# Attention with a split-precision score product: transposing q and k in float32 and splitting behind the transpose

## The chip, the cores and the metric

The kernel runs on one core of a Trainium2 chip. The core has five engines that run side by side and wait for each other by semaphores: TensorE (PE: matrix products, with its weight loads shown as PEld), VectorE (DVE), ScalarE (ACT), GpSimd (POOL) and SyncE (SP), which here only issues DMAs. Products land in PSUM, which only PE, DVE and ACT reach. The metric is the device time of one execution in microseconds, as the median of several runs; lower is better. A trace of one profiled execution shows when each instruction ran.

## The reference

Four sequences of 768 positions, eight heads of 64. Each position attends to the `n_global` = 8 first keys and to the `n_local` = 96 last ones, with a bias per head that falls with the distance; the result of all heads goes through a feed-forward network (FFN) with a rational function in the middle.

```python
scores = scale * np.matmul(q, k.transpose(0, 1, 3, 2))
keep = is_global | is_local          # key < 8, or 0 <= query - key < 96
bias = -slopes[:, None, None] * dist[None, :, :]
scores = np.where(keep, scores + bias, -1e9)
a = np.exp(scores - np.max(scores, axis=-1, keepdims=True))
a = a / (np.sum(a, axis=-1, keepdims=True) + 1e-09)
x = np.matmul(a, v)                  # heads side by side: 3072 tokens x 512
h = x @ w_in                         # 512 -> 2048
P = a[0] + a[1] * h + a[2] * h**2 + a[3] * h**3
Q = 1.0 + np.abs(b[0]) * np.abs(h) + np.abs(b[1]) * h**2
out = (P / (Q + 1e-06)) @ w_out      # 2048 -> 512
```

All data are float32; the weights arrive as 64-bit numbers and are decoded on the chip.

## The kernel before, in words

**Units and steps.** Attention is cut into 96 units (`unit`): 128 queries of one sequence and two heads, so four units to a block of 128 tokens. A window of 96 keys reaches no further back than the block before, so a unit's keys are its own block and the one before it (256 columns, in two halves of `kT` used in turn); the eight global keys are written over the first columns of the older half (`kG`, L409). The first block of a sequence, i = 0, has one half only. The FFN goes in chunks of 256 tokens, eight parts `f` to a chunk. The loop in `windowed` (L511) makes 110 steps `t`; each step takes up pieces of several units and FFN parts, with the FFN twelve steps behind (`LAG`) and its second product two more (`F2`). Within a step the order is set by the numbers in `PRI` and `PRI_A` (lower is earlier): scores 50, softmax 100, first half of the first FFN product 150, transposes of q and k 200, product with v 250, and so on. A scheduler turns these priorities and the dependencies into one instruction order per engine. Pairs of units share a load (`st_load`, every even step, two pairs ahead) and the product with v (`st_pv`, odd steps).

**Precision.** A product of type float32r (FR) keeps fewer bits than float32. So numbers are split: a high part rounded to FR and a low part, the rest. A product is then the sum of high by high, high by low and low by high; the FFN does this with three FR products per tile (L257, L333).

**Scores before.** `st_split` (L364) rounds q and k of a unit on VectorE (L368), subtracts on GpSimd (L369), and lays high and low part of one head beside each other, 64 + 64 columns. `st_qkT` (L372) transposes the four 128x128 tiles in FR (q and k, two heads) into the PSUM tile `tk`, so that partitions 0 to 63 hold a head's high part and 64 to 127 its low part. `st_qkE` (L384) takes them out on ScalarE: q with a scale per head (L391), k into `kT` (L394), the global keys into `kG` (L396). Two DMAs (L392, L393) then make a copy of q with high and low part exchanged. `st_score` (L399) makes two products of 128 rows per head (L407): q by k gives high by high plus low by low, the exchanged q by k gives the two mixed terms. For i = 0 the one half is read twice, so that the product still has 256 columns. The mask, the bias and the row's minimum come in one VectorE instruction per head (L418).

**After the scores.** `st_soft` (L423): one exponential per head on ScalarE (L428), then sum (L431) and reciprocal (L433) on VectorE; `st_norm` (L435) scales on GpSimd (L440); `st_pT` (L443) transposes in float32 (L450) and copies out (L452); `st_pv` (L455) multiplies with v, two heads side by side in 64 columns each (L467); `st_x` (L473) splits the result for the FFN (L486, L487). In PSUM, three tiles (`ps_t`, a bank each) go round among `tk`, the scores, `tp` and `o`.

**The beginning.** During the first 18 steps the weights are loaded (L162, in SP's queue) and decoded (`decode`, L157, most of it on VectorE) and from then on split (`split_w`); the first chunk of the FFN uses plain float32 (L249, L328).

Of the kernel before, what the change touches and what calls it, by code (L numbers as in the profile page):

```python
# [9 lines left out]
F32 = mybir.dt.float32  # L10
FR = mybir.dt.float32r
# [83 lines left out]
def tile_kernel(ctx: ExitStack, tc: tile.TileContext, q, k, v, n_global, n_local,  # L95
# [126 lines left out]
    stats = const.tile([P, 4, 8], F32, name="stats")  # L222

    def load_coef():
        nc.sync.dma_start(out=coef[:, 0:4], in_=ca.partition_broadcast(P))
# [119 lines left out]

    kT = const.tile([P, H, 2, P], FR, name="kT")
    kG = const.tile([P, H, G], FR, name="kG")
    ident = const.tile([P, P], F32, name="ident")  # L350
    ident_r = const.tile([P, P], FR, name="ident_r")
    mask0 = const.tile([P, P], F32, name="mask0")
    masks = const.tile([P, 3, P], F32, name="masks")
    sp = {}
    tqk = {}
    qTs = {}
    prob = {}
    pTs = {}
    ops = {}
# [1 line left out]
    def blocks_of(x, i):  # L361
        return x if i else x[..., 0, :]

    def st_split(u):  # L364
        p = unit(u)[2]
        n = nat[u // 2][:, :, 2 * (p % 2):2 * (p % 2) + 2, :]
        s = pl.att.tile([P, 2, 2, 2, D], FR, tag="split", name=f"sp{u}", bufs=1)
        nc.vector.tensor_copy(out=s[:, :, :, 0, :], in_=n)  # L368
        nc.gpsimd.tensor_tensor(out=s[:, :, :, 1, :], in0=n, in1=s[:, :, :, 0, :], op=ALU.subtract)  # L369
        sp[u] = s  # L370

    def st_qkT(u):  # L372
        s = sp.pop(u)
        tk = pl.ps_t.tile([P, 2, 2, P], FR, tag="t", name=f"tk{u}")
        for z in range(2):
            for x in range(2):
                nc.tensor.transpose(out=tk[:, z, x, :], in_=s[:, z, x].rearrange("p a d -> p (a d)"),  # L377
                                    identity=ident_r)
        tqk[u] = tk

    def st_qkE(u):  # L384
        c, t, p, b, i = unit(u)
        tk = tqk.pop(u)
        hs = slice(2 * p, 2 * p + 2)
        qT = pl.att.tile([P, 2, 2, P], FR, tag="qT", name=f"qT{u}", bufs=3)
        for x in range(2):

            nc.scalar.activation(out=qT[:, 0, x], in_=tk[:, 0, x], func=AF.Copy, scale=float(2.0 ** (2 * p + x - 2)))  # L391
        nc.sync.dma_start(out=qT[0:D, 1].bitcast(F32), in_=qT[D:P, 0].bitcast(F32))  # L392
        nc.sync.dma_start(out=qT[D:P, 1].bitcast(F32), in_=qT[0:D, 0].bitcast(F32))  # L393
        nc.scalar.copy(out=kT[:, hs, i % 2, :], in_=tk[:, 1])  # L394
        if i == 0:
            nc.scalar.copy(out=kG[:, hs, :], in_=tk[:, 1, :, 0:G])  # L396
        qTs[u] = qT

    def st_score(u):  # L399
        c, t, p, b, i = unit(u)  # L400
        qT = qTs.pop(u)
        s_ps = pl.ps_t.tile([P, 2, 2, P], F32, tag="t", name=f"s{u}")
        for x in range(2):
            h = 2 * p + x
            rhs = kT[:, h] if i else kT[:, h, 0:1, :].broadcast_to([P, 2, P])
            for z in range(2):
                nc.tensor.matmul(out=s_ps[:, x], lhsT=qT[:, z, x, :], rhs=rhs, start=(z == 0), stop=(z == 1))  # L407
        if 1 <= i < NT - 1:
            nc.gpsimd.tensor_copy(out=kT[:, 2 * p:2 * p + 2, i % 2, 0:G], in_=kG[:, 2 * p:2 * p + 2, :])  # L409
        if i == 0:  # L410
            mk = mask0
        else:
            mk = masks[:, 0:2, :] if i % 2 else masks[:, 1:3, :]
        pr = pl.att.tile([P, 2, 2, P], F32, tag="prob", name=f"pr{u}")
        st = stats[:, u % 4]
        for x in range(2):
            h = 2 * p + x
            nc.vector.tensor_tensor_reduce(  # L418
                out=blocks_of(pr[:, x], i), in0=blocks_of(s_ps[:, x], i), in1=mk,
                scale=-(2.0 ** -(h + 1)), scalar=3e38, op0=ALU.add, op1=ALU.min, accum_out=st[:, x:x + 1])  # L420
        prob[u] = (pr, st)

    def st_soft(u):  # L423
        i = unit(u)[4]
        pr, st = prob[u]
        for x in range(2):
            d = blocks_of(pr[:, x], i)
            nc.scalar.activation(out=d, in_=d, func=AF.Exp, scale=-1.0, bias=st[:, x:x + 1],  # L428
                                 accum_out=st[:, 2 + 2 * x:3 + 2 * x])

        nc.vector.tensor_reduce(out=st[:, 6:8], in_=st[:, 2:6].rearrange("p (x w) -> p x w", w=2), op=ALU.add,  # L431
                                axis=mybir.AxisListType.X)
        nc.vector.reciprocal(out=st[:, 6:8], in_=st[:, 6:8])  # L433

    def st_norm(u):  # L435
        i = unit(u)[4]
        pr, st = prob[u]
        for x in range(2):
            d = blocks_of(pr[:, x], i)
            nc.gpsimd.tensor_scalar(  # L440
                out=d, in0=d, scalar1=st[:, 6 + x:7 + x], scalar2=None, op0=ALU.mult)

    def st_pT(u):  # L443
        i = unit(u)[4]
        pr, st = prob.pop(u)
        W = 2 if i else 1
        t_ps = pl.ps_t.tile([P, 2, 2, P], F32, tag="t", name=f"tp{u}")
        for x in range(2):
            for w in range(W):
                nc.tensor.transpose(out=t_ps[:, x, w, :], in_=pr[:, x, w, :], identity=ident)  # L450
        pT = pl.att.tile([P, 2, 2, P], F32, tag="pT", name=f"pT{u}", bufs=2)
        (nc.scalar.copy if u < EARLY else nc.vector.tensor_copy)(out=pT[:, :, 0:W, :], in_=t_ps[:, :, 0:W, :])  # L452
        pTs[u] = pT

# [38 lines left out]
    def windowed():  # L493
        st_load(0)
        st_load(2)
        nc.sync.dma_start(out=ni[:, 0:2], in_=n_local.bitcast(I32).partition_broadcast(P))
        nc.sync.dma_start(out=ni[:, 2:4], in_=n_global.bitcast(I32).partition_broadcast(P))
        make_identity(nc, ident)
        nc.vector.tensor_copy(out=ident_r, in_=ident)
        nc.vector.tensor_copy(out=nf, in_=ni)  # L500
        load_coef()
        st_split(0)
        st_split(1)

        nl, ng = nf[:, 0:1], nf[:, 2:3]
        scr = tmp("scr").rearrange("p a (b w) -> p (a b) w", w=P)
        scr = [scr[:, x, :] for x in range(4)]
        window_masks(nc, scr, mask0, masks, nl, ng)

        base = tc.cur_priority  # L510
        for t in range(NU + LAG + F2):  # L511
            f = t - LAG
            pri = PRI_A if f < FPC else PRI

            def on(name, fn, u, *args):
# [4 lines left out]
            if t % 2 == 0:  # L520
                on("load", st_load, t + 4)
            on("score", st_score, t - 2)
            on("soft", st_soft, t - 2)
            on("ffn1a", st_ffn1, f, 0)
            on("qkT", st_qkT, t)
            if t % 2:
                on("pv", lambda u: st_pv(u // 2), t - 5)
            on("qkE", st_qkE, t)
            if t % 2:
                on("x", lambda u: st_x(u // 2), t - 5)  # L530
            if t:
                on("split", st_split, t + 1)
# [178 lines left out]
```

## Time and profile before

| | |
|---|---|
| median of 3 runs | 793.19 us (793.1 to 794.15) |
| the profiled execution | 793.47 us, its span 791.7 us |
| granted TensorE clock | 0.996 of full speed |
| scores, L407 | 384 products of 128x256, 70.2 us of PE |
| transposes of q and k, L377 | 384 of 128x128, 49.6 us of PE |
| transposes of the probabilities, L450 | 352 of 128x128, 63.0 us of PE |
| product with v, L467 | 704 of 64 columns by 128, 53.2 us of PE |
| copies of q, L392 and L393 | 192 DMAs, 2.1 us from issue to landing |

How to read it: the span runs from the first to the last instruction. Busy time of PE overlaps from one product to the next, since products are pipelined and their ends are modelled; the distance between two starts is what one costs in a full stream. A busy engine matters only where the chain of waits runs through it. A group row gives: line, engine, operation, output and inputs, shape, count, then busy us and mean ns of one, then the engine's idle time ahead of these instructions and who ended it.

### The profile page before, as it was taken

Reading aid. Unit: us, or ns where it says so; the run is one execution under the profiler, and the core shown is the slowest. Engines: PE = TensorE matmul, PEld = TensorE weight load, DVE = VectorE, ACT = ScalarE, POOL = GpSimd, SP = SyncE. Lnnn points to the kernel's source line nnn. Section 1 sums busy time; section 2 is a strip of 40 time slices with the busy share of each in tenths; the row PEclk is TensorE's granted clock in tenths of the full one; section 3 lists DMA queues with packets and bytes.
Section 4 is the critical chain, followed back from the end, with each engine's and each line's share of the span. In section 5 each row is a group of like instructions: output and inputs, shape, how many; then the busy total and the mean of one; then the engine's idle time right before and its main releaser. Section 6 shows DMA issues by size and latency. Waiting matters only on the chain.

```text
span 791.7 us, 15480 instructions
## 1 busy us (share of the span) xinstructions
PE 745.0 (94%) x5184; PEld 647.2 (82%) x5184; DVE 589.6 (74%) x1453; ACT 573.0 (72%) x1407; POOL 531.7 (67%) x572
## 2 busy tenths in 40 slices
PE   3678998899999999999999999999999999999995
PEld 2466656598988998988998988988998988988993
DVE  5899998988786767776776767776776767776664
ACT  4688767776786777777777777777777777776763
POOL 3887657998966676675676676675677676664440
PEclk9999999999999999999999999999999999999999
DMA  7884555122121222222222222222222222100000
GB/s 182 233 228 144 158 156 159 44 65 64 43 58 23 62 55 49 62 54 58 57 47 49 61 55 48 61 55 53 63 48 48 61 56 48 41 15 1 27 1 32
DMA packets 101400, 55.90 MB, mean 71 GB/s; under 512 B 81856, under 2 KB 94144, under 8 KB 101312
## 3 DMA queue, kind: packets, MB, share of 16 engines
q1 hardware_dynamic: 101312, 54.82, 26.3%
q8 instruction: 44, 0.72, 0.4%
q14 instruction: 44, 0.36, 0.1%
HBM read 35.92 MB, written 6.29 MB: 53 GB/s over the span
## 4 chain that ended last, share of the span: by engine, by line
PE 81%; DVE 9%; POOL 3%; DMA 2%; issue 2%; ACT 1%; SPq 0%; DVEq 0%; POOLq 0%; ACTq 0%
PE h L257 32%; PE acc L333 30%; PE s L407 5%; PE o L467 5%; PE tp L450 4%; PE tk L377 3%; POOL pr L440 2%; PE acc L328 1%; DMA qT<-qT 1%; DVE pr L418 1%; DMA r<-in_moe_w_out_dram 1%; DVE fu L304 1%; POOL sp L369 1%; DVE fu L288 1%; DVE r L189 1%
## 5 line engine op out<-in xcount | busy, mean ns | idle before, releaser
L333 PE MATMUL acc<-wout_h,g 128*128 128x512 f32 x704 | 250.1, 406 | 0.8 <-ACT g L312 0.8
L257 PE MATMUL h<-xh,win_h 128*128 128x256 f32 x704 | 204.7, 291 | 2.4 <-DVE fu L289 2.4
L440 POOL TENSOR_SCALAR pr<-pr,stats 128x256 f32<-128x256 f32 (+1 forms) x192 | 180.5, 950 | 32.9 <-DVE stats L433 15.5
L257 PE MATMUL h<-xl,win_h 128*128 128x256 f32 x704 | 197.7, 281 | 0.0
L290 POOL TENSOR_TENSOR fa<-fa,fs 128x512 f32<-128x512 f32 x95 | 124.5, 1311 | 91.1 <-ACT fs L283 87.3
L333 PEld LDWEIGHTS acc<-wout_h,g 128*128 128x128 f32 x704 | 128.5, 188 | 23.3 <-ACT g L312 1.2
L257 PEld LDWEIGHTS h<-xh,win_h 128*128 128x128 f32 x704 | 132.5, 188 | 11.3 <-issue 6.6
L369 POOL TENSOR_TENSOR sp<-nat,sp 128x256 fp32r<-128x256 f32 x96 | 75.9, 791 | 95.8 <-DVE sp L368 45.8
L257 PEld LDWEIGHTS h<-xl,win_h 128*128 128x128 f32 x704 | 132.4, 188 | 1.8 <-issue 0.5
L428 ACT ACTIVATE pr<-pr,stats 128x256 f32<-128x256 f32 (+1 forms) x192 | 92.6, 485 | 55.2 <-DVE stats L418 55.0
L281 ACT ACTIVATE fu<-h,coef 128x512 f32<-128x512 f32 (+1 forms) x97 | 75.0, 774 | 60.3 <-PE h L257 59.4
L313 POOL TENSOR_TENSOR g<-fu,g 128x512 fp32r<-128x512 f32 x87 | 112.7, 1295 | 7.9 <-DVE fu L289 4.5
L302 DVE SCALAR_TENSOR_TENSOR fu<-fu,coef,q 128x512 f32<-128x512 f32 (+1 forms) x97 | 71.6, 738 | 48.2 <-ACT q L298 47.2
L297 ACT ACTIVATE fs<-fa,coef 128x512 f32<-128x512 f32 (+1 forms) x97 | 69.6, 718 | 34.9 <-POOL fa L290 32.5
L452 DVE COPY pT<-tp 128x512 f32<-128x512 f32 (+1 forms) x75 | 48.5, 646 | 61.8 <-PE tp L450 61.2
L288 DVE TENSOR_TENSOR fu<-fu,h 128x512 f32<-128x512 f32 (+1 forms) x97 | 65.3, 673 | 12.3 <-ACT fs L283 10.7
L407 PE MATMUL s<-kT,qT 128*128 128x256 f32 x384 | 70.2, 304 | 4.4 <-DMA qT<-qT 3.4
L289 DVE SCALAR_TENSOR_TENSOR fu<-fu,coef,h 128x512 f32<-128x512 f32 (+1 forms) x97 | 71.8, 740 | 2.6
L450 PE MATMUL tp<-ident,pr 128*128 128x128 f32 x352 | 63.0, 282 | 10.7 <-POOL pr L440 10.2
L303 DVE SCALAR_TENSOR_TENSOR q<-fa,coef,q 128x512 f32<-128x512 f32 (+1 forms) x97 | 72.1, 743 | 0.0
L407 PEld LDWEIGHTS s<-kT,qT 128*128 128x128 f32 x384 | 60.4, 199 | 11.6 <-issue 2.4
L283 ACT ACTIVATE fs<-h,coef 128x512 f32<-128x512 f32 (+1 forms) x97 | 66.5, 685 | 0.1
(271 smaller groups left out, 1622.5 us busy)
## 6 DMA issues: line engine op xcount, KB each, us to landing
qT<-qT SPq DMA_DIRECT2D x192, 64.0 KB, 2.1
r<-in_moe_w_in_dram SPq DMA_DIRECT2D x16, 512.0 KB, 5.4
r<-in_moe_w_out_dram SPq DMA_DIRECT2D x16, 512.0 KB, 3.5
nat<-in_q_dram SPq DMA_DIRECT2D x48, 128.0 KB, 2.7
nat<-in_k_dram SPq DMA_DIRECT2D x48, 128.0 KB, 2.5
vt<-in_v_dram SPq DMA_DIRECT2D x48, 128.0 KB, 2.3
out_dram<-o SPq DMA_DIRECT2D x24, 256.0 KB, 2.1
vt<-in_v_dram SPq DMA_DIRECT2D x32, 8.0 KB
```

The costliest lines, as they stand in the source:

```text
L257: nc.tensor.matmul(out=hps[f][:, y, :], lhsT=w[:, fs], rhs=x[:, ct, :], start=(n == 0), stop=(n == 3 * NCT - 1))
L281: nc.scalar.activation(out=u, in_=h, func=AF.Identity, scale=a3, bias=a2)
L288: nc.vector.tensor_tensor(out=u, in0=u, in1=h, op=ALU.mult)
L290: side(f).tensor_tensor(out=a, in0=a, in1=s, op=ALU.add)
L303: nc.vector.scalar_tensor_tensor(out=r, in0=a, scalar=q1, in1=r, op0=ALU.add, op1=ALU.mult)
L313: side(f).tensor_tensor(out=g[:, 1, ys], in0=u, in1=g[:, 0, ys], op=ALU.subtract)
L333: nc.tensor.matmul(out=acc, lhsT=gs[f][:, z, y, ts], rhs=w, start=(ft == 0 and n == 0), stop=(ft == NFT - 1 and n == 2))
L369: nc.gpsimd.tensor_tensor(out=s[:, :, :, 1, :], in0=n, in1=s[:, :, :, 0, :], op=ALU.subtract)
L407: nc.tensor.matmul(out=s_ps[:, x], lhsT=qT[:, z, x, :], rhs=rhs, start=(z == 0), stop=(z == 1))
L428: nc.scalar.activation(out=d, in_=d, func=AF.Exp, scale=-1.0, bias=st[:, x:x + 1], accum_out=st[:, 2 + 2 * x:3 + 2 * x])
L440: nc.gpsimd.tensor_scalar(out=d, in0=d, scalar1=st[:, 6 + x:7 + x], scalar2=None, op0=ALU.mult)
L450: nc.tensor.transpose(out=t_ps[:, x, w, :], in_=pr[:, x, w, :], identity=ident)
```

## The change

The split moves behind the transpose. q and k of four heads (a load's worth) are transposed as they are, in float32, four tiles in all; on leaving PSUM, ScalarE writes the high parts (q with its scale per partition from the new `qs`) and VectorE writes the low parts. A transposed tile now holds two heads, one in partitions 0 to 63 and one in 64 to 127, and `kT` holds high and low part in tiles of their own. The scores of a head are three products of 64 rows, those of two heads in turn, into two PSUM tiles, one for each of the two heads. The copies of q by DMA, `st_split` and the exchange are gone; for i = 0 the product has 128 columns. Transposes, scores and softmax work on four heads: transposes in odd steps, scores and softmax in the even step behind. Sum and reciprocal are taken once for four heads. `prob` and `pT` get a third buffer. `kG` is written by GpSimd.

```diff
+    kT = const.tile([P, NPAIR, 2, 2, P], FR, name="kT")
+    qs = const.tile([P, NPAIR], F32, name="qs")
...
-    def st_split(u):
...
-        nc.vector.tensor_copy(out=s[:, :, :, 0, :], in_=n)
-        nc.gpsimd.tensor_tensor(out=s[:, :, :, 1, :], in0=n, in1=s[:, :, :, 0, :], op=ALU.subtract)
...
+    def st_qkT(m):
+        n = nat[m]
+        tk = pl.ps_t.tile([P, 2, 2, P], F32, tag="t", name=f"tk{m}")
         for z in range(2):
+            for y in range(2):
+                nc.tensor.transpose(out=tk[:, z, y, :], in_=n[:, z, 2 * y:2 * y + 2, :].rearrange("p a d -> p (a d)"),
+                                    identity=ident)
+        tqk[m] = tk
+
+    def st_qkE(m):
+        p, i = of_pairs(m)
+        tk = tqk.pop(m)
+        qT = qTs[m] = pl.att.tile([P, 2, 2, P], FR, tag="qT", name=f"qT{m}")
+        kh, kl = (kT[:, p:p + 2, z, i % 2, :] for z in range(2))
+        for y in range(2):
+            nc.scalar.activation(out=qT[:, 0, y], in_=tk[:, 0, y], func=AF.Identity, scale=qs[:, p + y:p + y + 1])
+        nc.scalar.copy(out=kh, in_=tk[:, 1])
+        for y in range(2):
+            nc.vector.scalar_tensor_tensor(out=qT[:, 1, y], in0=tk[:, 0, y], scalar=qs[:, p + y:p + y + 1],
+                                           in1=qT[:, 0, y], op0=ALU.mult, op1=ALU.subtract)
+        nc.vector.tensor_tensor(out=kl, in0=tk[:, 1], in1=kh, op=ALU.subtract)
+        if i == 0:
+            nc.gpsimd.tensor_copy(out=kG[:, p:p + 2], in_=kT[:, p:p + 2, :, 0, 0:G])
+
+    def st_score(m):
+        p, i = of_pairs(m)
+        qT = qTs.pop(m)
+        sx = [pl.ps_t.tile([P, 2, 2, P], F32, tag="t", name=f"s{x}_{m}") for x in range(2)]
+        for y in range(2):
+            for n, (zq, zk) in enumerate(((0, 0), (0, 1), (1, 0))):
+                for x in range(2):
+                    r = slice(x * D, (x + 1) * D)
+                    nc.tensor.matmul(out=blocks_of(sx[x][:, y], i), lhsT=qT[r, zq, y, :],
+                                     rhs=blocks_of(kT[r, p + y, zk], i), start=(n == 0), stop=(n == 2))
...
-        for x in range(2):
-
-            nc.scalar.activation(out=qT[:, 0, x], in_=tk[:, 0, x], func=AF.Copy, scale=float(2.0 ** (2 * p + x - 2)))
-        nc.sync.dma_start(out=qT[0:D, 1].bitcast(F32), in_=qT[D:P, 0].bitcast(F32))
-        nc.sync.dma_start(out=qT[D:P, 1].bitcast(F32), in_=qT[0:D, 0].bitcast(F32))
-        nc.scalar.copy(out=kT[:, hs, i % 2, :], in_=tk[:, 1])
...
+    def st_soft(m):
+        i = of_pairs(m)[1]
+        st = stats[:, m % 4]
+        for n in range(4):
+            d = blocks_of(prob[2 * m + n // 2][:, n % 2], i)
+            nc.scalar.activation(out=d, in_=d, func=AF.Exp, scale=-1.0, bias=st[:, n:n + 1],
+                                 accum_out=st[:, 4 + 2 * n:5 + 2 * n])
+        nc.vector.tensor_reduce(out=st[:, 12:16], in_=st[:, 4:12].rearrange("p (x w) -> p x w", w=2), op=ALU.add,
+                                axis=mybir.AxisListType.X)
+        nc.vector.reciprocal(out=st[:, 12:16], in_=st[:, 12:16])
...
+            if not odd:
                 on("load", st_load, t + 4)
-            on("score", st_score, t - 2)
-            on("soft", st_soft, t - 2)
+                on_m("score", st_score, m - 1)
+                on_m("soft", st_soft, m - 1)
             on("ffn1a", st_ffn1, f, 0)
...
+            if odd:
+                on_m("qkT", st_qkT, m)
+                on_m("pv", st_pv, m - 2)
+                on_m("qkE", st_qkE, m)
+                on_m("x", st_x, m - 2)
```

More of the change, by code (lines that the diff above doesn't have):

```diff
@@ L399, in st_score @@
[L399 to L402, printed above, removed]
-        for x in range(2):
[L404 to L441, printed above, removed]
+    def of_pairs(m):
+        c, t, p, b, i = unit(2 * m)
+        return p, i
+    def st_qkT(m):
+        n = nat[m]
+        tk = pl.ps_t.tile([P, 2, 2, P], F32, tag="t", name=f"tk{m}")
+        for z in range(2):
+            for y in range(2):
+                nc.tensor.transpose(out=tk[:, z, y, :], in_=n[:, z, 2 * y:2 * y + 2, :].rearrange("p a d -> p (a d)"),
+                                    identity=ident)
+        tqk[m] = tk
@@ L443, in st_pT, with st_norm @@
+    def st_norm(u):
+        m, y = divmod(u, 2)
+        i = of_pairs(m)[1]
+        for x in range(2):
+            d = blocks_of(prob[u][:, x], i)
+            nc.gpsimd.tensor_scalar(out=d, in0=d, scalar1=stats[:, m % 4, 12 + 2 * y + x:13 + 2 * y + x],
+                                    scalar2=None, op0=ALU.mult)
     def st_pT(u):
         i = unit(u)[4]
-        pr, st = prob.pop(u)
+        pr = prob.pop(u)
         W = 2 if i else 1
@@ L498, in windowed @@
         make_identity(nc, ident)
-        nc.vector.tensor_copy(out=ident_r, in_=ident)
+        for p in range(NPAIR):
+            for x in range(2):
+                nc.gpsimd.memset(qs[x * D:(x + 1) * D, p:p + 1], 2.0 ** (2 * p + x - 2))
         nc.vector.tensor_copy(out=nf, in_=ni)
         load_coef()
-        st_split(0)
-        st_split(1)
         nl, ng = nf[:, 0:1], nf[:, 2:3]
```

54 lines of the change are left out of this document (20 added, 34 removed).

## The prediction

> **What bounds the kernel now.** I read the page first (busy time, then the chain of waits that ended last), then busy time by stretches, then TensorE's timeline over two steps, then the groups by line.
>
> ```profile
> span 791.7 us, 15480 instructions
> ...
> PE 745.0 (94%) x5184; PEld 647.2 (82%) x5184; DVE 589.6 (74%) x1453; ACT 573.0 (72%) x1407; POOL 531.7 (67%) x572
> ...
> PE 81%; DVE 9%; POOL 3%; DMA 2%; issue 2%; ACT 1%; SPq 0%; DVEq 0%; POOLq 0%; ACTq 0%
> PE h L257 32%; PE acc L333 30%; PE s L407 5%; PE o L467 5%; PE tp L450 4%; PE tk L377 3%; POOL pr L440 2%; PE acc L328 1%; DMA qT<-qT 1%; DVE pr L418 1%; DMA r<-in_moe_w_out_dram 1%; DVE fu L304 1%; POOL sp L369 1%; DVE fu L288 1%; DVE r L189 1%
> ```
>
> TensorE holds 81% of the chain; the lines that the change touches on it are s (L407, 5%) and tk (L377, 3%). Is that an average over unlike stages? Busy time by stretches says yes (columns: stretch, its length, then busy us of PE, weight loads, DVE, ACT, POOL):
>
> ```profile
> 0.00:40.00 40.00, 19.11 (x92) 14.53 (x93) 28.68 (x108) 23.03 (x79) 24.56 (x37) 1.00 0.79 209
> 40.00:80.00 40.00, 33.05 (x203) 25.70 (x203) 38.11 (x103) 33.23 (x89) 31.27 (x34) 1.00 0.64 182
> 80.00:120.00 40.00, 37.43 (x194) 24.53 (x193) 38.14 (x94) 28.45 (x69) 23.15 (x26) 1.00 0.57 162
> 120.00:160.00 40.00, 33.67 (x198) 23.93 (x197) 38.37 (x78) 30.00 (x72) 35.83 (x30) 0.96 0.34 102
> 320.00:400.00 80.00, 80.00 (x588) 72.22 (x588) 56.15 (x148) 60.03 (x155) 52.89 (x57) 1.00 0.25 62
> ```
>
> There are two stages. Up to about 160 us (weights arriving and being decoded) VectorE is full: 38 of each 40 us from 40 us on. After that PE has no gap at all (80.00 of 80.00) and the others have a quarter or more to spare. So in the second stage the change is worth what it takes from TensorE's stream, to the microsecond; in the first, what it takes from VectorE and from the waits.
>
> How much of the attention lies in which stage, from the score products alone (PE's and the weight loads' counts are the x numbers):
>
> ```profile
> 0.00:80.00 80.00, 15.73 (x56) 11.26 (x56) 9.71 (x28) 1.00 0.72 196
> 80.00:160.00 80.00, 7.07 (x37) 5.17 (x38) 6.81 (x18) 0.98 0.45 132
> ```
>
> 93 of 384 products by 160 us, four to a unit of two heads: 23 of 96 units. In what follows a pair is two units, which is four heads. So 11.5 pairs lie in the VectorE stage and 36.5 in the TensorE stage.
>
> **The change part by part, on TensorE.** A busy PE row overlaps with the next one, so I cost by distances between starts. These are PE's rows from two steps (start us, length of the merged group, operation, count):
>
> ```profile
> 500.78 0.60 PE L450 MATMUL tp<-ident,pr 128*128 128x128 f32 x4
> 501.14 0.51 PE L333 MATMUL acc<-wout_h,g 128*128 128x512 f32 x1
> 501.48 0.40 PE L333 MATMUL acc<-w_12l,g 128*128 128x512 f32 x1
> ...
> 502.42 0.39 PE L333 MATMUL acc<-wout_h,g 128*128 128x512 f32 x1
> 502.65 0.65 PE L407 MATMUL s<-kT,qT 128*128 128x256 f32 x4
> 503.13 0.28 PE L257 MATMUL h<-xh,win_h 128*128 128x256 f32 x1
> 503.25 0.28 PE L257 MATMUL h<-xl,win_h 128*128 128x256 f32 x1
> ...
> 504.55 0.46 PE L377 MATMUL tk<-ident_r,sp 128*128 128x128 f32 x4
> 504.94 1.09 PE L467 MATMUL o<-pT,vt 128*64 128x128 f32 x16
> 505.96 0.39 PE L257 MATMUL h<-xh,win_h 128*128 128x256 f32 x1
> 506.19 0.28 PE L257 MATMUL h<-xl,win_h 128*128 128x256 f32 x1
> ...
> 512.59 0.46 PE L377 MATMUL tk<-ident_r,sp 128*128 128x128 f32 x4
> 512.89 0.35 PE L257 MATMUL h<-xh,win_h 128*128 128x256 f32 x1
> 513.07 0.28 PE L257 MATMUL h<-xl,win_h 128*128 128x256 f32 x1
> ```
>
> Scores now: 503.13 - 502.65 = 0.48 us for four products of 256 columns, 0.12 each, the rate of L257 too (503.25 - 503.13). A pair has eight: 0.96 us.
>
> Transposes now: four reduced-precision ones per unit. In the even step they stand alone: 513.07 - 512.59, less one ordinary product (0.12), is 0.36 us. In the odd step they stand ahead of the value products (L467). The change has four transposes per pair, in float32, in the odd step only. The nearest row is L450, float32 transposes of the same shape: its group of four lasts 0.60 against 0.46 for L377's. So the even step loses 0.36 us and the odd one gains 0.60 - 0.46 = 0.14: a saving of 0.22 us per pair.
>
> New scores: per pair twelve products with 64 rows, 256 columns each, ordered head by head, so that each two neighbours use the upper and the lower half of the array and write different PSUM tiles. Nothing in this trace uses half the rows, so the price has bounds. The nearest row is L467, products with 64 columns of the array, two heads side by side: 16 take 505.96 - 504.94 = 1.02 us. What would they take one after the other?
>
> ```profile
> L467 PE MATMUL o<-pT,vt 128*64 128x128 f32 x704 | 53.2, 284 | 1.6 <-ACT pT L452 1.6
> ...
> L249 PE MATMUL h<-x,w_0f 128*128 128x256 f32 x32 | 7.4, 385 | 0.0
> ```
>
> L249, float32 with 256 columns, is 7.4/32 = 0.231 us of PE each; 128 columns would be some 0.115 (an estimate, its half), and 16 of those 1.85 us. They take 1.02, so two do run at once. If half rows do the same, six couples at 0.12 are 0.72 us; if they don't, twelve at 0.12 are 1.44.
>
> The weight loads of the two:
>
> ```profile
> L407 PEld LDWEIGHTS s<-kT,qT 128*128 128x128 f32 x384 | 60.4, 199 | 11.6 <-issue 2.4 <-DMA qT<-qT 2.1 <-ACT kT L394 0.8
> ...
> L467 PEld LDWEIGHTS o<-pT,vt 128*64 128x64 f32 x704 | 39.0, 138 | 9.7 <-issue 1.9 <-ACT pT L452 1.7 <-DVE stats L418 1.2
> ```
>
> PE's rows also show a price for going into and out of such a burst. Into it: L377's start to L467's is 0.39 us against 0.30 when an ordinary product follows (512.89 - 512.59), so 0.09. Out of it: from 504.94 to the second product after the burst (506.19) are 1.25 us, where eight couples at 0.115 and one product at 0.12 make 1.04, so 0.21. Sum 0.30 us. The loads of L467 are narrower than those of the scores (138 against 199 ns), and as the first load of a burst stands uncovered I add 0.05: 0.35. The bounds are 0 (L333 to L407 now takes 502.65 - 502.42 = 0.23 us, an ordinary L333 spacing) and 0.45. I take 0.35, as L467 is the one row with two tiles.
>
> On this the Trainium skill ("TensorEngine Tiling (Array Packing)", Key Properties) speaks against the change: it says that going from one tiling mode to another drains the engine. The L467 rows agree for half columns (0.30 us); no run here shows it yet for half rows, and by the rule the sum is the one with 0.35, by the L333-to-L407 row the one with 0.
>
> So a pair's scores go from 0.96 to 0.72 + 0.35 = 1.07 us: +0.11. With the transposes: +0.11 - 0.22 = -0.11 us per pair, and 36.5 pairs make -4.0 us. In the first block of a sequence (six of these pairs) the new products have 128 columns instead of 256. The couple then costs between 0.07 (a quarter of L377's 0.30) and 0.23 (L249's price, if narrow products lose the fast rate); I take 0.12 as before, with -1.8 to +4.0 us as its ends (six pairs by six couples by -0.05 or +0.11).
>
> **The other engines.** Rows by group (busy us, mean ns of one):
>
> ```profile
> L369 POOL TENSOR_TENSOR sp<-nat,sp 128x256 fp32r<-128x256 f32 x96 | 75.9, 791 | 95.8 <-DVE sp L368 45.8 <-DVE stats L431 33.8 <-DVE stats L433 6.6
> ...
> L391 ACT ACTIVATE qT<-tk 128x128 fp32r<-128x128 f32 x192 | 41.1, 265 | 14.1 <-PE tk L377 13.6 <-ACT w_0f L170 0.4
> ...
> L368 DVE CAST sp<-nat 128x256 fp32r<-128x256 f32 x96 | 36.0, 375 | 39.3 <-POOL kT L409 13.7 <-PE tk L377 11.4 <-POOL g L313 7.1
> L394 ACT CAST kT<-tk 128x256 fp32r<-128x256 f32 x96 | 35.7, 372 | 0.0
> ...
> L487 DVE TENSOR_TENSOR xl<-o,xh 128x256 fp32r<-128x256 f32 x44 | 18.3, 417 | 3.1 <-ACT xh L486 3.1
> ...
> L433 DVE RECIPROCAL stats<-stats 128x2 f32<-128x2 f32 x96 | 15.2, 158 | 1.1
> L431 DVE TENSOR_REDUCE stats<-stats 128x2 f32<-128x4 f32 x96 | 14.4, 151 | 12.0 <-ACT pr L428 11.9
> ...
> L418 DVE CUSTOM_DVE_ANT_0 pr<-s,mask 128x128 f32<-128x128 f32 x32 | 8.0, 284 | 0.3
> ```
>
> VectorE per pair: out go two casts (2 x 0.375) and one of two reduce and reciprocal pairs (0.31); in come the low part of k (as L487: 0.417) and two of q, 128x128 out of PSUM (as L418's small form: 2 x 0.284). That is 0.985 - 1.06 = -0.08 us, a draw. ScalarE: L391 and L394 halve, -38 us over the run. POOL: L369 goes, -76 us; eight small kG copies come to it, and the kG writes of L409 halve in number. All of this lies beside TensorE in the second stage and is worth nothing there. What would it cost uncovered? Nothing grows but VectorE's k and q parts, 48 x 0.985 = 47 us, and VectorE has 24 of 80 us free in that stage.
>
> In the first stage, the chain of waits of the first 160 us has the removed steps in it: the copies of qT, and L369.
>
> ```profile
> 51.91 3.20 DMA qT<-qT
> ...
> 57.16 2.98 DMA qT<-qT
> ```
>
> These two rows are 6.2 us, and they lie before 62 us, where the stretch view has VectorE idle for 11.3 of the first 40 us. From there on it is full with decoding, which doesn't change, so what attention gains early is mostly waited for again. VectorE's own saving there is 11.5 x 0.08 = 0.9 us. Bounds: -7 us (both copies and that saving), +3 (11.5 x 0.985 = 11.3 us of new VectorE work against 8.6 of removed casts, if the fewer reductions save nothing). I take -2.
>
> **Waits that the change adds.** The loads of q and k (L131, L132) now wait for transposes in the next odd step instead of for the split: some half a step later, and behind them in SP's queue stand the v loads, L470, the output and, early, the weights (L162). The loads are issued four steps ahead, some 32 us at 8.0 us a step (L377's 512.59 - 504.55), so this is covered; two qT copies per unit leave the same queue. Scores take two of three PSUM tiles at once until four masks have run on VectorE, and four exponentials now come in one step on ScalarE:
>
> ```profile
> L428 ACT ACTIVATE pr<-pr,stats 128x256 f32<-128x256 f32 (+1 forms) x192 | 92.6, 485 | 55.2 <-DVE stats L418 55.0
> ```
>
> ScalarE is busy for 60.03 of 80 us in the second stage, 6.0 of an 8.0 us step; two more exponentials with their reads make it some 7.2 in even steps, and less in odd ones; the normalised rows are needed a step later. So it is covered, with 0.8 us to spare; uncovered, each even step would wait for the excess.
>
> **The sum.** Against the profiled execution (793.47 us, its span 791.7): -4.0 - 2.0 gives 787.5. The median of the runs is 0.28 lower, 793.19, so 787.2: I say 787.
>
> **Rivals.**
> *Cheap entry.* Half rows need no drain: six couples at 0.72 alone, -0.24 - 0.22 = -0.46 per pair, -16.8 us; with -2, 774.4. For it: now, nothing is lost between L333 and L407. Against: L467's burst.
> *Half rows don't overlap* (slower). The two loads of a couple take turns at a quarter of L377's 0.36, so 0.18 us a couple: 1.08 + 0.35 - 0.96 - 0.22 = +0.25, +9 us, 800; or the products themselves take turns: 1.44 + 0.35 - 1.18 = +0.61, +22 us, 813. It decides from 0.138 us a couple on (6 x 0.138 + 0.35 = 1.18). For it: 64-row operands are nowhere in this trace. Against: L467's 1.02 us. The Trainium skill ("TensorE: Matmul & The Clock Gate", Part 3) has tiles in different row groups start some 4 ns apart; no run here shows that for rows, and by it this rival falls.
> *No gain.* The burst costs 0.45 and the first stage is pinned by VectorE: -0.01 per pair, 793.
> *New wait.* ScalarE's four exponentials push the FFN's evictions out in the even steps: 0.3 us in each of 36 is +11 us, with the sum's -6 making 798.
>
> **Chances.** Forecast 0.40, cheap entry 0.20, no gain 0.15, no overlap 0.19, new wait 0.06. A measurement here can tell 0.2% (1.6 us) from no change: faster 0.60, same 0.15, slower 0.25. The range 773 to 801 takes in the first block's ends and all but the 813 case. The forecast's own range is 782 to 791.
>
> **What would show it.** Right: L377's successor with 192 float32 transposes and a group of four near 0.60; twelve score products in 0.72 + 0.35 us from first start to the second product behind them; PE still 80.00 of 80.00 in the middle stretches; step pairs 0.11 us shorter. Wrong: the twelve near 0.72 with no loss around them (cheap entry) or over 1.2 (no overlap); idle PE at the head of even steps (new wait); a second stage that starts at another time than 158 to 160 us, which would put the first stage's term wrong.

## The result and the profile after

The change makes the kernel slower: 821.21 us (median of 4 runs, 820.67 to 823.37) against 793.67 us for the kernel before, timed beside it (4 runs, 793.1 to 794.82). The ratio is 1.035, with a 95% interval of 1.0327 to 1.0374, so +27.5 us. Forecast were 787 us and a range of 773 to 801: the sign is wrong, and the time lies outside the range.

The page after, with the span, the busy times and the chain of waits that ended last:

```profile
span 821.6 us, 14599 instructions
...
PE 771.6 (94%) x5184; PEld 641.8 (78%) x5184; DVE 585.2 (71%) x1407; ACT 550.8 (67%) x1244; POOL 450.3 (55%) x460
...
PE 82%; DVE 8%; DMA 3%; ACT 2%; POOL 2%; issue 2%; SPq 1%; POOLq 0%; DVEq 0%; ACTq 0%
PE h L257 32%; PE acc L333 30%; PE s L404 7%; PE o L462 5%; PE tp L445 4%; DMA r<-in_moe_w_in_dram 2%; PE tk L375 2%; POOL pr L435 1%; PE acc L328 1%; DVE pr L414 1%; DMA r<-in_moe_w_out_dram 1%; DVE r L189 1%; DVE q L303 1%; DVE fu L288 1%; DVE fu L304 1%
```

VectorE, ScalarE and GpSimd all have less to do than before (by 4, 22 and 81 us), and none has taken the bound: TensorE still holds 82% of the chain. The instruction count of TensorE is the same, 5184, yet it is busy for 27 us more. Busy time by stretches after:

```profile
0.00:40.00 40.00, 16.21 (x84) 10.84 (x86) 26.02 (x104) 20.84 (x61) 15.95 (x36) 1.00 0.70 195
40.00:80.00 40.00, 27.42 (x165) 20.70 (x163) 36.51 (x87) 27.71 (x68) 16.77 (x18) 1.00 0.55 163
80.00:120.00 40.00, 40.00 (x173) 26.04 (x174) 39.20 (x85) 27.54 (x59) 23.80 (x19) 0.96 0.42 127
120.00:160.00 40.00, 37.05 (x215) 25.92 (x214) 33.41 (x74) 26.63 (x61) 27.01 (x24) 0.96 0.26 74
...
320.00:400.00 80.00, 80.00 (x571) 68.93 (x569) 55.47 (x135) 53.30 (x122) 44.78 (x47) 1.00 0.15 36
```

In the middle PE is full as before, 80.00 of 80.00, but gets 571 instructions done there where it did 588. A full engine that does less: so the extra time has to lie between the starts of its own products. The rows show it. TensorE after, one pair's scores first, then transposes, value products, and the next pair's scores (start us, length of the merged group, operation, count):

```profile
493.68 0.97 PE L404 MATMUL s<-kT,qT 64*128 64x256 f32 x6
494.57 0.73 PE L333 MATMUL acc<-wout_h,g 128*128 128x512 f32 x2
...
497.00 0.39 PE L333 MATMUL acc<-wout_h,g 128*128 128x512 f32 x1
497.24 0.39 PE L333 MATMUL acc<-w_6l,g 128*128 128x512 f32 x1
497.55 0.98 PE L404 MATMUL s<-kT,qT 64*128 64x256 f32 x6
498.46 0.38 PE L257 MATMUL h<-xh,win_h 128*128 128x256 f32 x1
498.68 0.29 PE L257 MATMUL h<-xl,win_h 128*128 128x256 f32 x1
...
503.71 0.60 PE L375 MATMUL tk<-ident,nat 128*128 128x128 f32 x4
...
506.60 0.66 PE L462 MATMUL o<-pT,vt 128*64 128x128 f32 x8
507.18 0.39 PE L257 MATMUL h<-xh,win_h 128*128 128x256 f32 x1
507.50 0.66 PE L462 MATMUL o<-pT,vt 128*64 128x128 f32 x8
508.09 0.39 PE L257 MATMUL h<-xl,win_h 128*128 128x256 f32 x1
...
513.09 0.39 PE L333 MATMUL acc<-wout_h,g 128*128 128x512 f32 x1
513.32 0.39 PE L333 MATMUL acc<-w_10l,g 128*128 128x512 f32 x1
513.64 0.97 PE L404 MATMUL s<-kT,qT 64*128 64x256 f32 x12
514.54 0.73 PE L333 MATMUL acc<-wout_h,g 128*128 128x512 f32 x2
```

The burst at 513.64 is as the code is written: twelve products, the two heads in turn, and 0.90 us to the next start. The pair before it was torn: six products of one head at 493.68, FFN products, and six of the other head at 497.55. Each half takes 0.89 to 0.91 us, as long as all twelve, since two heads can't share the array when they don't meet. The value products at 506.60 are torn as well, by a single FFN product at 507.18.

**The price of a burst**, from the same rows. In: 513.64 - 513.32 = 0.32, against 0.23 between the FFN products ahead of it, so 0.09. Inside: 0.90 less six couples at 0.118 (0.71) leaves 0.19, which lies at its first couple and behind its last. Out: the second product behind a burst comes late, 498.68 - 498.46 = 0.22 instead of 0.12, so 0.10. Together 0.38; the median over whole score bursts that stand in a stream of FFN products, here and in the kernels below, is 0.39 to 0.40. For the value products it is 0.35: eight of them take 0.59 us from first start to the next product behind, sixteen 1.02, so 0.11 a couple, and the rest of such a burst is its way in and out. By the Trainium skill ("TensorEngine Tiling (Array Packing)", Key Properties) a change of tiling mode drains the engine; these rows agree, for half rows as for half columns.

In the planned instruction order of TensorE, the scores of the 48 pairs stand in 77 bursts after the change, and only 16 of them are the twelve in turn; 31 are sixes of one head. Of the 190 couples in the eight chunks of the table below, 120 ran side by side. The value products stand in 78 bursts, where the kernel before had 57.

### The profile page after: what moved, and what is told of

It is laid out like the page before. It is cut to its first block, busy times and chain, and to the rows that moved or that the text cites. A ratio compares the mean times of both kernels' runs of the same rounds, so it can differ in the third digit from the quotient of the medians.

```text
span 821.6 us, 14599 instructions
## 1 busy us (share of the span) xinstructions
PE 771.6 (94%) x5184; PEld 641.8 (78%) x5184; DVE 585.2 (71%) x1407; ACT 550.8 (67%) x1244; POOL 450.3 (55%) x460
## 3 DMA queue, kind: packets, MB, share of 16 engines
q1 hardware_dynamic: 85952, 42.22, 18.8%
## 4 chain that ended last, share of the span: by engine, by line
PE 82%; DVE 8%; DMA 3%; ACT 2%; POOL 2%; issue 2%; SPq 1%; POOLq 0%; DVEq 0%; ACTq 0%
PE h L257 32%; PE acc L333 30%; PE s L404 7%; PE o L462 5%; PE tp L445 4%; DMA r<-in_moe_w_in_dram 2%; PE tk L375 2%; POOL pr L435 1%; PE acc L328 1%; DVE pr L414 1%; DMA r<-in_moe_w_out_dram 1%; DVE r L189 1%; DVE q L303 1%; DVE fu L288 1%; DVE fu L304 1%
## 5 line engine op out<-in xcount | busy, mean ns | idle before, releaser
L333 PE MATMUL acc<-wout_h,g 128*128 128x512 f32 x704 | 241.3, 405 | 0.8 <-ACT g L312 0.8
L435 POOL TENSOR_SCALAR pr<-pr,stats 128x256 f32<-128x256 f32 (+1 forms) x192 | 174.7, 925 | 122.3 <-DVE stats L428 88.9
L257 PE MATMUL h<-xl,win_h 128*128 128x256 f32 x704 | 201.2, 286 | 0.0
L333 PEld LDWEIGHTS acc<-wout_h,g 128*128 128x128 f32 x704 | 127.1, 188 | 25.3 <-ACT g L312 1.3
L257 PEld LDWEIGHTS h<-xh,win_h 128*128 128x128 f32 x704 | 132.5, 188 | 15.2 <-issue 6.5
L414 DVE CUSTOM_DVE_ANT_0 pr<-s,masks 128x256 f32<-128x256 f32 x160 | 60.1, 420 | 21.7 <-PE s L404 18.2
L404 PE MATMUL s<-kT,qT 64*128 64x256 f32 (+1 forms) x576 | 70.4, 309 | 1.6 <-ACT kT L386 1.0
L404 PEld LDWEIGHTS s<-kT,qT 64*128 64x128 f32 x576 | 55.0, 199 | 21.6 <-issue 11.9
L445 PEld LDWEIGHTS tp<-ident,pr 128*128 128x128 f32 x352 | 43.5, 143 | 33.1 <-POOL pr L435 20.1
```

The lines of the kernel that those rows point to most:

```text
L257: nc.tensor.matmul(out=hps[f][:, y, :], lhsT=w[:, fs], rhs=x[:, ct, :], start=(n == 0), stop=(n == 3 * NCT - 1))
L333: nc.tensor.matmul(out=acc, lhsT=gs[f][:, z, y, ts], rhs=w, start=(ft == 0 and n == 0), stop=(ft == NFT - 1 and n == 2))
L404: nc.tensor.matmul(out=blocks_of(sx[x][:, y], i), lhsT=qT[r, zq, y, :], rhs=blocks_of(kT[r, p + y, zk], i), start=(n == 0), stop=(n == 2))
L435: nc.gpsimd.tensor_scalar(out=d, in0=d, scalar1=stats[:, m % 4, 12 + 2 * y + x:13 + 2 * y + x], scalar2=None, op0=ALU.mult)
```

## The experiments

Two theories were put up. **Order**: the scheduler tears the bursts, each part pays the change of mode again, and torn heads lose their overlap. **Rival**: something of the change as such costs, whatever the order: half rows, float32 transposes, or four heads at a time. Each kernel was timed beside the kernel before on its own chip; the medians of that one were 794.1 us for the first four kernels and 794.57 us for the other four.

The profiles can be cut at the copies of FFN output (from PSUM to SBUF): up to the first copy of the second chunk, from there over eight chunks to the first copy of the tenth, and the rest. Times in us; the granted clock was 1.00 over the eight chunks in all six, but not in the beginning:

| kernel | beginning (granted clock) | eight chunks | rest | bursts in the eight chunks: scores, value products |
|---|---|---|---|---|
| before | 218.5 (0.992) | 469.2 | 104.0 | full products, 34 |
| the change | 223.2 (0.985) | 493.2 | 105.2 | 48, 54 |
| couples | 226.0 (0.955) | 481.8 | 106.6 | 39, 50 |
| both_whole | 217.3 (0.961) | 482.7 | 104.6 | 40, 39 |
| before_v_split | 215.4 (0.984) | 478.8 | 106.8 | full products, 63 |
| full_rows | 211.2 (0.976) | 467.8 | 101.0 | full products, 36 |

The eight chunks don't hold quite the same work in each kernel: the count of FFN products of 256 columns differs by up to 35, which is 4.1 us at 0.118 each.

**1. Scores held together (couples).** The second head's PSUM bank came last, from the value products; so its product goes first and waits for their evacuation, and the twelve keep their order.

```diff
-                for x in range(2):
+                for x in (1, 0):
...
+                    if (y, n, x) != (0, 0, 1):
+                        tc.keep_in_program_order(mm)
+                    elif freed:
+                        tc.add_manual_dep(mm.ins, freed[0].ins.name, ...)   # freed: evacuation of o, st_x
```

> Order theory: in the changed kernel the scheduler took the two heads' score products apart (they are written head by head, but run as six of one head and six of the other in many pairs, so the two half arrays do not run together) and put FFN products between, and each way into and out of a tiled burst costs about 0.39 us. Over eight chunks of the trace 72 of 192 couples were broken (72 x 0.118 = 8.5 us) and there were 16 score bursts too many (6.2 us); over the whole run that is some 17 us. This kernel keeps the twelve products in order and lets them start only when the PSUM tiles of both heads are free; the products with v are left as they are. Order theory: 821 - 17 = 804 us. Rival one (the half-row products and float32 transposes are dearer by themselves, whatever their order): 817 to 821. Rival two (waiting for two PSUM tiles at once stalls TensorE): above 821, with PE idle in the middle stretches.

Measured: 815.81 us (813.9 to 816.52), ratio 1.0259 (1.0215 to 1.0304). Over the eight chunks it takes 481.8 us where the change takes 493.2; there 194 of its 197 couples run side by side, where the change had 120 of 190. But its beginning is 2.8 us longer, with two units fewer scored by its end, and the rest 1.4 us longer. That the waiting for both banks costs this is not shown, as the granted clock was lower there too. In the planned order, turning the heads round alone leaves only 14 whole bursts; with the wait there are 36, with or without the fixed order. So, in the planned order, it is in the main the late bank that tears a pair.

**2. Scores and value products held together (both_whole).** As 1, and in `st_pv` the second unit's products go first and keep their order.

```diff
-        for y in range(2):
+        for y in (1, 0):
...
+                    if (y, n, x) != (1, 0, 0):
+                        tc.keep_in_program_order(mm)
```

> As the kernel with kept couples, and the products with v of four heads are kept in one burst too (54 bursts over eight chunks in the changed kernel, 34 in the one before: 20 x 0.39 = 7.8 us, over the run 9). Order theory: 795 us, about as the kernel before, since what is left is the price of one score burst per pair (0.72 + 0.39 against 0.96) less the cheaper transposes (0.22 per pair). Rival one: 817 to 821. Rival two: above 821.

Measured: 806.39 us (805.55 to 807.43), ratio 1.0148 (1.0105 to 1.0191). So mending the bursts is worth 15.2 of the 27.5 us, 5.8 with the scores held together and 9.4 more with the value products. But that isn't what each costs: over the eight chunks the scores alone bring 11.4 us and the value products nothing to be seen (481.8 and 482.7, some 2 us better when the unequal work is taken out), while most of the 9.4 lies in the beginning, 226.0 against 217.3, where the order of the work and the granted clock differ. What the beginning owes to the bursts stays open. A whole burst here:

```profile
504.07 0.98 PE L405 MATMUL s<-kT,qT 64*128 64x256 f32 x12
504.97 0.38 PE L257 MATMUL h<-xl,win_h 128*128 128x256 f32 x1
505.19 0.28 PE L257 MATMUL h<-xh,w_0l 128*128 128x256 f32 x1
```

From 504.07 to 504.97 are 0.90 us, and 0.22 - 0.12 = 0.10 behind it. But with most of its bursts mended (38 of 48 pairs whole in the planned order) the change is still 12.3 us slower than the kernel before: order isn't all.

**3. Whole, but one head after the other (whole_serial).** As 2, with the loop over heads outside.

```diff
-        for y in range(2):
-            for n, (zq, zk) in enumerate(((0, 0), (0, 1), (1, 0))):
-                for x in (1, 0):
+        for x in (1, 0):
+            for y in range(2):
+                for n, (zq, zk) in enumerate(((0, 0), (0, 1), (1, 0))):
```

> As the kernel with both bursts whole, but within a score burst all six products of one head come first and then all six of the other. If half rows of different heads run together only when they are neighbours, this costs 6 x 0.118 us in each of 36.5 pairs, 26 us more than the kernel with both bursts whole: 821 us if that one is at 795. If couples do not matter (rival one), the two are equal.

Measured: 823.04 us, ratio 1.0357 (1.0301 to 1.0413), 16.7 over both_whole. So sharing the array is worth 0.35 us a pair even against this. The expected loss was 26 us. TensorE's rows show why it is less:

```profile
512.57 1.32 PE L405 MATMUL s<-kT,qT 64*128 64x256 f32 x12
513.82 0.39 PE L257 MATMUL h<-xl,win_h 128*128 128x256 f32 x1
```

The twelve take 1.25 us, not the 12 x 0.118 + 0.19 = 1.61 of single file: in the middle of the burst three pairs of starts lie 2 to 6 ns apart, so some products of the second head did run beside the first head's. In the planned order this burst is six of one head and then six of the other.

**4. The kernel before with torn value products (before_v_split).** The price in a kernel that has nothing else of the change: `st_pv` is cut in two, one unit each, with the first FFN half between.

```diff
+PRI = dict(..., pv=140, ..., pv2=250)
-                on("pv", lambda u: st_pv(u // 2), t - 5)
+                on("pv", lambda u: st_pv(u // 2, 0), t - 5)
...
+                on("pv2", lambda u: st_pv(u // 2, 1), t - 5)
```

> The kernel before with the products with v of four heads in two bursts instead of one, with other TensorE work between (37 more bursts in TensorE's instruction list; nothing else changed). If a burst's way in and out costs 0.39 us: 793.5 + 14 = 808 us. If the bursts are free and only the new products are dear (rival one): 793.5 to 795 us.

Measured: 802.43 us (801.79 to 802.79), ratio 1.0095 (1.0059 to 1.0131): +8.3 us with the same products. In the eight chunks there are 63 bursts instead of 34 and 478.8 us instead of 469.2, so 9.6 / 29 = 0.33 us for each burst more; that stretch also holds some 2.3 us of other work more (an estimate from the counts and prices of its products), and without it the price is 0.25. Over the whole run it is 8.3 / 37 = 0.22. The direction is as expected; the price is less than the 0.39 expected, and nearer to the 0.35 of the value products' rows.

**5. No change of mode (full_rows).** As 2, but each couple is one product of all 128 rows: six at the same rate, ordinary mode. This sums two heads and leaves the low parts out of one sum, so the scores aren't the reference's.

```diff
-            for n, (zq, zk) in enumerate(((0, 0), (0, 1), (1, 0))):
-                for x in (1, 0):
-                    mm = nc.tensor.matmul(out=..., lhsT=qT[r, zq, y, :], rhs=blocks_of(kT[r, p + y, zk], i), ...)
+            for x, terms in ((1, ((0, 0), (0, 1))), (0, ((1, 0),))):
+                for n, (zq, zk) in enumerate(terms):
+                    mm = nc.tensor.matmul(out=..., lhsT=qT[:, zq, y, :], rhs=blocks_of(kT[:, p + y, zk], i), ...)
```

> As the kernel with both bursts whole (806.4 us), but the scores are six products of all 128 rows per pair instead of six couples of 64 rows: this sums two heads and leaves the low parts out of one, so the scores are not the reference's; TensorE streams the same six times 256 columns. Order theory: what a couple burst loses is the way into and out of the tiled mode, 0.39 us a burst, and 8 of the 40 score bursts in eight chunks are fragments: 806.4 - 36.5 x 0.39 - 9 x 0.39 = 789 us. If changing the mode costs nothing and the loss is elsewhere: 806.

Measured: 782.25 us (781.82 to 782.69), ratio 0.9837 (0.9815 to 0.986). It keeps all else: float32 transposes, VectorE's low parts, four heads at a time, two banks, and the time that six couples take. Besides the mode, it has six products and six weight loads fewer per pair. It is 24 us faster than both_whole. Its rows have no loss on the way in and out:

```profile
512.65 0.39 PE L333 MATMUL acc<-wout_h,g 128*128 128x512 f32 x1
512.88 0.87 PE L405 MATMUL s<-kT,qT 128*128 128x256 f32 x6
513.59 0.60 PE L452 MATMUL tp<-ident,pr 128*128 128x128 f32 x4
...
528.77 0.78 PE L405 MATMUL s<-kT,qT 128*128 128x128 f32 x6
529.39 0.33 PE L257 MATMUL h<-xh,win_h 128*128 128x256 f32 x1
```

0.23 from L333 into the burst, and six products in 0.71 us. The six products fewer don't explain it: six couples inside a burst take the same 0.118 us each, and what a burst loses lies at its two ends. So going over to half rows and back is what turns the change, once its bursts are mended, from a gain into a loss: 24.6 us by the differences to the kernel before. Over the 58 score bursts that both_whole has in its planned order that is 0.42 us each; over the eight chunks it is 14.9 us for 40 bursts, 0.37 each. Both are near the 0.39 of the rows. The rival that the other parts cost is refuted for their sum.

Why only 12.3 us faster than before, and not 18.8? TensorE is no longer quite full in this kernel. What it waited for after 160 us (engine, line, releaser: us in total, times, longest):

```profile
PE h L257 <- DVE fu L289: 4.0, 8, 1.8
PE acc L333 <- ACT g L312: 1.3, 1, 1.3
PE tp L452 <- ACT pT L454: 0.6, 1, 0.6
PE tp L452 <- DVE pT L454: 0.2, 1, 0.2
```

That is 6.1 us, where the kernel before waits for 2.4 us in the same stretch. With its own work shortened, TensorE begins to meet the FFN's rational function on VectorE. That is 3.7 of the 6.5 us missing; the rest isn't placed.

**6. The kernel before with float32 transposes (before_f32_transposes).** Only the type of L377's transposes changes.

```diff
-        tk = pl.ps_t.tile([P, 2, 2, P], FR, ...)
+        tk = pl.ps_t.tile([P, 2, 2, P], F32, ...)
-                nc.tensor.transpose(out=tk[:, z, x, :], in_=..., identity=ident_r)
+                nc.tensor.transpose(out=tk[:, z, x, :], in_=....bitcast(F32), identity=ident)
```

> The kernel before with its eight transposes of q and k per pair done as float32 (the same split data, the same places). It prices the float32 transpose by itself: 0.46 - 0.36 = 0.10 us for the four in the even step and 0.14 for the four in the odd one, 0.24 per pair, 36.5 pairs: +9, 803 us. If a float32 transpose costs no more than a reduced-precision one: 794.

Measured: 806.95 us (806.78 to 807.12), ratio 1.0148 (1.0125 to 1.0171): +12.4 us for 384, 0.032 us each. The rows give less: a group of four that stands among FFN products takes 0.07 us more (0.44 for 0.37, its way out included), one ahead of the value products 0.13 (0.53 for 0.40), which makes 48 x 0.20 = 9.6 us. The granted clock was also lower in this run's profile, 0.984 against 0.996, all of it outside the eight chunks. The change halves their number; at this rate its 192 transposes cost at most 6.2 us more than in FR, less than the 17 us of the 192 that went (48 groups of four at the 0.36 us of the prediction). This term was no part of the loss.

**7. Transposes one step earlier (early_transposes).** In both_whole, attention is behind at the first output copy (20 units scored at 160.4 us, where the kernel before has 23 at 156.5). One idea was that the low parts on VectorE, between transposes and scores, take a further turn through a full queue. So `st_qkT` and `st_qkE` move from odd steps to the even steps ahead.

```diff
-            if odd:
+            if not odd:
                 on_m("qkT", st_qkT, m)
                 on_m("qkE", st_qkE, m)
+            if odd:
                 on_m("pv", st_pv, m - 2)
```

> As the kernel with both bursts whole, with transposes and their split one step earlier (even step), so that the split on VectorE lies two steps ahead of the scores, as the split of the kernel before did. Theory of the first stage: in the changed kernel attention is 4 units behind the kernel before when the first chunk is done (20 of 23 units' scores, 15.3 of 19.6 units' value products), because the split became a further turn through a full VectorE queue inside each pair's chain, and the 4 units of 1.9 us are made up later: 7.5 us. Then this kernel gives 799. Rival: attention falls behind for another reason (four heads going through together), then 806.

Measured: 812.69 us, ratio 1.022 (1.0195 to 1.0245): slower than both_whole by 6 us. The units scored at the first copy rise to 22, but the copy comes at 165.5 us. Not supported. full_rows has that further turn too and brings its first copy at 148.8 us.

**8. Value products and scores in one stretch (bursts_joined).** Both use half the array; side by side they might pay the way in and out once. `st_pv` and `st_x` move ahead of the scores, the value products wait until all operands are there, and the transposes of the probabilities of both units move into the odd step.

```diff
+PRI = dict(..., pv=40, ..., x=110, ...)      # in the even step, pv ahead of the scores at 50
...
+                    else:
+                        tc.add_manual_dep(mm.ins, freed[0].ins.name, ...)   # freed: low part of k
...
-            on("pT", st_pT, t - 3)
+            if odd:
+                on("pT", st_pT, t - 3)
+                on("pT", st_pT, t - 2)
```

> As the kernel with both bursts whole, with the products with v directly ahead of the scores in the even step, in one fixed order (both transposes of probabilities then lie in the odd step), so that per pair there is one way into and one out of tiled work and no fragments (48 and 48 bursts in TensorE's list, all whole). Order theory: the 13 fragments per eight chunks go (13 x 36.5/32 x 0.39 = 5.8 us) and between 0.2 and 0.39 us of each pair's 0.78 of mode changes (7 to 14 us): 787 to 793. If the changes of mode were not what costs: 806 or more, as the transposes of probabilities are now closer to their use.

Measured: 841.39 us (838.14 to 842.71), ratio 1.0567 (1.054 to 1.0595). A new wait took over; TensorE's largest, over the whole run:

```profile
PE tp L448 <- POOL pr L438: 52.3, 32, 9.5
PE h L257 <- DVE fu L289: 9.6, 8, 1.8
```

With value products and scores tied together and the transposes moved, the transposes of the probabilities stand behind GpSimd's scaling for 52 us. So the total says nothing about the mode; the rows do. The joined burst of a pair takes 1.93 us to the next product, as long as the two apart (1.02 and 0.90); saved are the second product behind the one and the way into the other, some 0.20 us. That is less than a whole price, since half columns to half rows is a change of mode as well: 0.20 us pass between the last value product and the first score, and the first couple still takes 0.16 to 0.23.

## Why the prediction was wrong, point by point

**The step that failed** is the one that put the new scores as one burst a pair, "ordered head by head, so that each two neighbours use the upper and the lower half of the array". That is the order of the code. The order on the engine is made by the scheduler, and with three banks for four users it kept only 16 of 48 pairs whole and in turn, and tore value products with them. No rival named this; mending most of it was worth 15.2 us (both_whole).

**The forecast against the runs.** Without a way in and out it had -18.8 us (its case of 774.4); full_rows, the same stream in ordinary mode, has -12.3. For the way in and out it had 0.35 x 36.5 = +12.8; taking it away was worth 24.6. For torn bursts it had 0; measured 15.2. The three misses, 6.5 + 11.8 + 15.2, are the 33.5 us between -6.0 and +27.5. They are differences between whole runs, with the unlike beginnings of the table in them.

**The sum again with the prices of the rows**, over the eight chunks, change against before: 70 couples apart at 0.118 are 8.3 us, 48 score bursts at 0.39 are 18.7, and 20 value bursts more at 0.35 are 7.0. Against them stand two products saved in each of 32 pairs (0.24 us a pair, 7.7) and the cheaper transposes (0.22, 7.0). That makes +19.3 us. Measured are +24.0, of which some 5.6 are other work that this stretch holds more after the change (an estimate from the counts and prices of its products), so +18.4. There the bursts explain the loss.

**The price of a burst** was nearly right: 0.35 against 0.39. What was wrong was the number. It was charged to the 36.5 pairs of the second stage alone, as if TensorE's time were free before 160 us, and to one burst a pair. In the first stage PE is at 40.00 of 40 from 80 to 120 us now, and both_whole stands 6 us behind full_rows at the first output copy of the second chunk, with two units fewer scored. So to charge nothing for TensorE in the first stage looks wrong. That the price alone does all of this there is not shown: between 40 and 80 us TensorE's granted clock was 0.87 in both_whole, 0.91 in full_rows and 1.00 in the change itself, and the order of the beginning differs from kernel to kernel.

**The first stage's -2 us** leaned on a misread line: the two copies of q, at 51.91 and 57.16 us, don't lie in the first 40 us, where VectorE was idle for 11.3, but in the 40 behind them, where it was busy for 38.11. In the runs the change's beginning is 4.7 us longer than before, not shorter.

**Couples run at once**: right. Starts within a couple lie 1 to 3 ns apart in the burst at 513.64, couples 0.118 apart. So the rival "half rows don't overlap" is wrong, although a torn pair costs what it would: 0.89 to 0.91 us for six products alone.

**Transposes**: a group of four lasts 0.60 as said, and the saving of 0.22 us a pair agrees with the rows: 0.44 for one group of float32 transposes now (0.53 to the value products behind it, less 0.09 for their way in), where the two groups before took 0.37 and 0.30, so 0.23.

**Narrow products of the first block**: 0.07 to 0.23 bounded, 0.12 taken. In full_rows six of 128 columns take 529.39 - 528.77 = 0.62 us, 0.10 each; the change's own couples of 128 columns start 0.11 apart in the burst at 189.80. Both are near the value taken, and half the columns save little.

**Other engines**: VectorE -4.4 us (-3.8 worked out), GpSimd -81 (-76), ScalarE -22 (-38; in part because q's activation takes 363 ns where the old one took 265). After the first stage all of this is hidden, as said.

**New waits**: after 160 us, TensorE waits in the change for 1.8 us on VectorE and 0.8 on ScalarE, 2.6 in all. The four exponentials and the later loads stayed covered. That wait rival didn't come.

**What stays open** is why the first two chunks lose as much as they do: the further turn through VectorE isn't it (early_transposes), and four heads at a time isn't it by itself, since full_rows has that and is early. The granted clock of the beginning differs from run to run as well. A start with the kernel before's order was not tried.

## What to carry to other kernels

Half-array products paid a fixed price here each time the stream went over to them and back: 0.39 us for row halves, or some three full products of 256 columns; a burst of six couples that saves two full products can't earn that. Count bursts, not products, and count them in the order that the scheduler makes of the code, with the PSUM banks that it has: two tiles that must be open at once were torn apart here when their banks came free at different times. Where the engine that bounds is full before and after, look at the distances between its starts first; waits and busy times showed nothing of this.

## What the hardware showed beyond that

The way out of a score burst is as dear as the way in (0.09 and 0.10 each way), and half of it falls on the second product behind it (0.22 instead of 0.12), which a look at the burst's own rows misses. Going from half columns to half rows costs about as much as from a full product (0.20 us, then a slow first couple of 0.16 to 0.23). Products of two row halves in one stretch needn't be neighbours in the planned order to overlap (whole_serial: 1.25 us for 1.61; over its eight chunks 81 of 190 couples ran side by side).
